# Quarter loads of two MLP weights, and engine orders written out as lists, in a fused attention and MLP kernel

## The chip, the cores and the metric

The kernel runs on one core of a Trainium2 chip. The metric is the device time of one execution in microseconds (us); for a kernel that was run several times it is the median. A profile is one execution recorded by the hardware profiler. PE is the matrix engine (TensorE), with a queue of its own for weight loads (PEld); ACT, DVE and POOL are the scalar, vector and GpSimd engines; SP is the sync engine, which here issues nearly all DMA transfers, one after another in its queue.

## The reference

Input x has 2048 rows of 448. Two branches are computed from it and mixed by a gate per row.

```python
g = sigmoid((x * gate_w).sum(-1, keepdims=True))
a = attention(x, wq, wk, wv, beta) @ wo      # 16 heads of 28, 4 segments of 512 rows, masked softmax,
                                             # mixed with a linear memory of the segments before
h = layernorm(x)
u = gelu(einsum('bsd,sf->bdf', h, w1) + b1)  # w1: 2048 x 1792
y = einsum('bdf,fs->bds', u, w2) + b2        # w2: 1792 x 2048
out = g * a + (1 - g) * y.transpose(0, 2, 1)
```

The MLP mixes rows, not columns: its weights w1 and w2 run over the 2048 rows. They are some 7.3 MB each and are the largest inputs.

## The kernel before

**Two products.** `mm1(ft)` (lines 1055 to 1080) computes one of 14 blocks of 128 hidden units: 16 matmuls named u{ft}-0 to u{ft}-15, one for each tile of 128 rows of x, summed in one bank of PSUM; ACT and DVE then apply the gelu. `mm2(T)` (lines 1082 to 1098) computes one of 16 blocks of 128 output rows: 14 matmuls y{T}-0 to y{T}-13 over the hidden blocks; DVE mixes the result with the attention branch and SP writes it out. The last block is split in two by columns.

**The ring of slots.** Weights come through three slots in SBUF of 4096 columns each. `ring_load` (lines 569 to 584) fills the next one: loads w1_0 to w1_6 bring 256 columns of w1 for all 16 row tiles (1024 KB in pieces of 512 bytes, enough for two values of ft), loads w2_0 to w2_7 bring 256 columns of w2 for all 14 tiles (896 KB, two values of T). Each load is one DMA with one semaphore of its own. A slot has one resource, `R_slot[r]` (line 517): a load waits until the last matmul that reads the slot's former content is through, and the first matmul of a chain waits until the whole load has landed. The w1 loads also wait, by `reads=R_wv` (line 578), for the load of wv.

**Other traffic in SP's queue.** SP also issues the loads of x and of the other weights, transposes of x from DRAM (line 538), transposes of phi(k) within SBUF (line 781, named tk), and the gathers of the fourth group of heads: `gather` writes rows of the projected k and q to a scratch tensor in DRAM, spare_heads (line 755, names gk and gq), and reads them back into other partitions (line 760). The scores of a segment's last heads need the rows read back; for the first two segments these reads are gq0_h0, gk0_h0, gk0_h1, gq0_h1 and gq0_h2, and the first scores that wait for them are sc1_2 (line 954).

**Attention.** `scores` fills the banks 0 to 3 with logits (line 954, names sc), ACT takes their exponential (line 963), POOL masks them (line 966). `pv_unit` computes a unit's product with v (line 990, names pv) and, behind the first segment, the memory's product (names mem); DVE transposes both out of PSUM (line 1004 for mem, named tm; line 1006 for pv, named ta). ACT's line 816 (named gt) reads the gate's column from the bank of the v projection (names prt).

**The order of the work.** Every operation is recorded by `Sched.op` with what it reads and writes. `Sched.plan` (lines 157 to 278) then simulates the engines with given costs and priorities (shifted by the table SHIFTS) and so sets the order of each engine's instructions and the bank that each user of the four free PSUM banks (4 to 7) gets: the one that came free first. `finalize` (line 280) works out the waits: an instruction waits for the engines and DMAs that it depends on, unless an earlier wait of its engine implies that. A wait beyond the first of an instruction is an instruction of its own (line 323). In a run of matmuls that holds one on 32 columns, the matmuls of 128 columns are issued as four of 32 columns (lines 329 to 333).

Of the kernel before, what the change touches and what calls it, by code (L numbers as in the profile page):

```python
# [17 lines left out]
NT = 16  # L18
# [3 lines left out]
NFT = 14  # L22
# [41 lines left out]
SWITCH = 97.0  # L64
# [10 lines left out]
class Sched:  # L75
# [13 lines left out]
    def op(self, eng, fn, reads=(), writes=(), name=None, dma=False, out=False, cost=100.0, prio=0.0, mode="f",  # L89
           nbytes=0, rel=0.0, port=False, take=None, use=(), alt=None,  # L90
# [27 lines left out]
        if dma:  # L118
            self._dma_uid += 1
            o.evspace = "dma_u%d" % self._dma_uid  # L120
            o.is_event = True
# [35 lines left out]
    def plan(self, shifts=()):  # L157

        import bisect

        shifts = dict(shifts)
        for o in self.ops:
            o.prio = (o.prio[0] + shifts.get(o.name.split("-")[0], 0.0), o.idx)
        succ = [[] for _ in self.ops]
        left = [0] * len(self.ops)
        ready = [o.rel for o in self.ops]
        for o in self.ops:
            for d in {x.idx: x for x in o.deps + o.order}.values():
                succ[d.idx].append(o)
                left[o.idx] += 1  # L170
        free = {e: 0.0 for e in ENGINES}
        mode = "f"
        chan = 0.0
        port = 0.0
        waiting = {e: [] for e in ENGINES}
        avail = {e: [] for e in ENGINES}
        banks = {p: {b: (0.0, []) for b in v} for p, v in self.pool.items()}
        for p, v in self.later.items():
            banks[p].update({b: (1e18, []) for b in v})

        def push(o):
            for e in o.alts:
                bisect.insort(waiting[e], (ready[o.idx], o.prio, o))

        for o in self.ops:
            if left[o.idx] == 0:
                push(o)
        line = []
        while len(line) < len(self.ops):
            best = None  # L190
            for e in ENGINES:
                w, a = waiting[e], avail[e]
                t = free[e]
                while w and w[0][0] <= t:
                    _, p, o = w.pop(0)
                    if o.start is None:
                        bisect.insort(a, (p, o))
                a[:] = [x for x in a if x[1].start is None]
                w[:] = [x for x in w if x[2].start is None]
                while True:  # L200
                    pick = None
                    can = [o for p, o in sorted(a + [(x[1], x[2]) for x in w if x[0] <= t])
                           if not o.take or sum(v[0] <= t for v in banks[o.take[0].pool].values()) >= len(o.take)]
                    if can:
                        pick = can[0]
                        if e == "PE":

                            if mode != "f":
                                lead = [o.prio for o in can if o.tile == "f"][:1]
                                tiled = [o for o in can if o.tile == "r" or o.tile == "h" and ([o.prio] <= lead or not lead)]  # L210
                                tiled = [o for o in tiled if o.tile == mode] + tiled
                                pick = tiled[0] if tiled else pick
                            elif pick.tile == "h":
                                rest = [o for o in can if o.tile == "f"]
                                if rest and not any(o.tile == "r" for o in can) and t < ready[pick.idx] + pick.hold:
                                    pick = rest[0]
                        break
                    nxt = [x[0] for x in w if x[0] > t][:1]
                    if a or w:
                        nxt += [v[0] for p in banks.values() for v in p.values() if t < v[0] < 1e12]  # L220
                    if not nxt:
                        break
                    t = min(nxt)
                if pick is not None and (best is None or t < best[0]):
                    best = (t, e, pick)
            t, e, o = best
            for g in o.take:
                pool = banks[g.pool]
                b = min((v[0], b) for b, v in pool.items())[1]
                g.bank = b  # L230
                o.deps = o.deps + pool[b][1]
                pool[b] = (1e18, [])
            o.eng = e
            o.fn, c, pt = o.alts[e]
            if o.evspace is None:
                o.evspace = e
            if e == "PE" and t < COLD:
                c *= 2.0
            if e == "PE" and o.tile != mode:
                c += SWITCH  # L240
                mode = o.tile
            if pt:
                t = max(t, port)
                port = t + c
            o.start = t
            o.cost = c
            free[e] = t + c
            if o.nbytes:
                chan = max(chan, t + 1090.0) + o.nbytes / 290.0
                o.end = max(t + 1900.0, chan + 850.0)  # L250
            else:
                o.end = t + c + LAT[e]
            for g in o.free:
                g.left -= 1
                g.users.append(o)
                if g.left == 0:
                    banks[g.pool][g.bank] = (max(x.end + hop(x.eng, "PE") for x in g.users), g.users)
            o.pos = len(line)
            line.append(o)
            self.per_eng[e].append(o)  # L260
            for x in succ[o.idx]:
                isdep = any(d is o for d in x.deps)
                r = (o.end + min(hop(e, y) for y in x.alts)) if isdep else free[e]
                if ready[x.idx] < r:
                    ready[x.idx] = r
                left[x.idx] -= 1
                if left[x.idx] == 0:
                    push(x)
# [9 lines left out]
        return max(o.end for o in line)  # L278
# [69 lines left out]
def pool_cost(n):  # L348
# [5 lines left out]
SHIFTS = (  # L354
# [29 lines left out]
def build_kernel(nc, X, WQ, WK, WV, WO, BETA, W1, B1, W2, B2, GW, OUT):  # L384
# [839 lines left out]
```

## Time and profile before

| what | us |
|---|---|
| median of 3 runs | 178.38 |
| lowest and highest run | 178.17, 179.44 |
| the profiled execution | 178.57 |
| its span, first to last instruction | 176.8 |
| PE busy | 169.7 |
| DVE busy | 149.6 |
| ACT busy | 134.1 |
| POOL busy | 69.2 |

The granted PE clock was 1.000 over the span. The profile's page gives the busy time and number of instructions of each engine, the DMA issues with their time to landing, and groups of instructions by source line. Other views of the trace are a table of busy time by stretch of time, a list of who waited for whom, and the timeline. In the list of waits a row reads: engine and line that stood idle, after the arrow what released it, then total us, number of waits and the longest. In the timeline a row reads: start, duration, engine, line, operation, tiles written and read, number of instructions merged into the row, and idle time before it with its releaser. A q behind an engine's name means its queue: an issue or a wait, not computation. A DMA's duration in SP's timeline is the time that the queue was held by issuing it; its landing is told apart from that.

### The profile page before, as it was taken

The page shows a single profiled execution, that of the slowest core. Times are in us where ns is not written, and L with a number is a line of the kernel's source. Part 1 is how long each engine was busy: PE and PEld are TensorE (multiplying, and loading weights), DVE is VectorE, ACT ScalarE, POOL GpSimd, SP SyncE. Part 2 cuts the span into 40 slices and gives each one's busy share as a digit, 9 for nine tenths or more (in the row PEclk, how much of TensorE's full clock was granted, in tenths as well). Part 3 has the DMA queues.
Part 4 walks back from the last instruction along what each step waited for, and adds up shares of the span by engine and source line. Part 5 has one row for each costly group of instructions (what it writes and reads, how often), then busy time and mean ns, then how long its engine had stood idle before and what let it go on. Part 6 is the DMA issues. An engine that isn't in the chain of part 4 may idle for free.

```text
span 176.8 us, 5552 instructions
## 1 busy us (share of the span) xinstructions
PE 169.7 (96%) x2354; PEld 81.8 (46%) x2354; DVE 149.6 (85%) x337; ACT 134.1 (76%) x170; POOL 69.2 (39%) x93
## 2 busy tenths in 40 slices
PE   8699999999999999999999999999999999999993
PEld 3343443345544544444544344444444544555652
DVE  6499999799995898998999999997889999992222
ACT  2277898999689999999999999987878877405100
POOL 8003016542302233437745644359474425450000
PEclk9999999999999999999999999999999999999999
DMA  6979983699939915852007360203938600166511
GB/s 153 281 142 304 259 158 84 167 302 193 245 78 268 240 35 161 192 171 46 4 11 201 77 170 22 61 28 95 224 99 227 170 8 4 56 176 194 153 59 52
DMA packets 49752, 24.62 MB, mean 139 GB/s; under 512 B 14256, under 2 KB 49488, under 8 KB 49728
## 3 DMA queue, kind: packets, MB, share of 16 engines
q1 hardware_dynamic: 49440, 24.05, 56.6%
q8 instruction: 18, 0.29, 0.7%
q10 hardware_dynamic: 288, 0.23, 0.6%
q14 instruction: 6, 0.05, 0.1%
HBM read 18.76 MB, written 2.36 MB: 119 GB/s over the span
## 4 chain that ended last, share of the span: by engine, by line
PE 78%; ACT 6%; DVE 6%; DMA 4%; SPq 3%; issue 2%
PE t L332 67%; PE t L954 6%; PE t L990 4%; DMA t<-in_A_wk_dram 3%; ACT t L963 2%; SPq L760 1%; SPq L755 1%; DVE t L913 1%; PE t L840 1%; DMA t<-spare_heads 1%; ACT t L1076 1%; ACT t L1065 1%; ACT t L1047 1%; DVE t L1071 1%; DVE t L1073 1%
## 5 line engine op out<-in xcount | busy, mean ns | idle before, releaser
L332 PE MATMUL t<-t 128*32 128x448 bf16 (+10 forms) x1620 | 145.8, 347 | 2.8 <-DVE t L649 1.7
L332 PEld LDWEIGHTS t<-t 128*32 128x32 bf16 (+2 forms) x1620 | 66.6, 97 | 68.6 <-issue 15.1
L963 ACT ACTIVATE t<-t 128x2048 bf16<-128x2048 f32 x40 | 76.2, 1904 | 6.3 <-PE t L954 6.1
L966 POOL TENSOR_SCALAR_AFFINE_SELECT t<-t 128x512 bf16<-128x512 bf16 x64 | 46.8, 732 | 58.2 <-ACT t L963 54.4
L1093 DVE SCALAR_TENSOR_TENSOR t<-t 128x448 bf16<-128x448 f32 (+2 forms) x17 | 10.9, 653 | 12.8 <-PE t L332 12.8
L1021 POOL TENSOR_TENSOR t<-t 128x448 bf16<-128x448 f32 x12 | 14.6, 1219 | 9.7 <-DVE t L1019 9.1
L1047 ACT ACTIVATE t<-t 128x448 bf16<-128x448 f32 x12 | 8.5, 732 | 10.3 <-PE t L332 10.1
L954 PE MATMUL t<-t 28*128 28x512 bf16 (+3 forms) x256 | 15.8, 301 | 0.3 <-DMA t<-spare_heads 0.3
L906 POOL TENSOR_TENSOR t<-t 128x4 f32<-128x4 f32 x4 | 4.5, 1130 | 20.9 <-DVE t L904 20.9
L1006 DVE STREAM_TRANSPOSE t<-t 128x512 f32<-128x512 f32 x16 | 11.2, 701 | 0.9 <-PE t L990 0.9
L990 PE MATMUL t<-t 128*32 128x256 bf16 (+3 forms) x256 | 11.5, 299 | 0.4 <-ACT t L816 0.4
L954 PEld LDWEIGHTS t<-t 28*128 28x128 bf16 x256 | 4.5, 92 | 14.1 <-ACT t L963 6.9
L1027 DVE STREAM_TRANSPOSE t<-t 128x512 bf16<-128x512 bf16 x16 | 10.9, 687 | 0.0
L1073 DVE SCALAR_TENSOR_TENSOR t<-t 128x448 f32<-128x448 f32 x14 | 8.8, 636 | 1.5 <-ACT t L1068 1.5
L1076 ACT ACTIVATE t<-t 128x448 f32<-128x448 f32 x14 | 8.5, 612 | 1.8 <-DVE t L1073 1.8
L1065 ACT ACTIVATE t<-t 128x448 f32<-128x448 f32 x14 | 9.3, 674 | 0.7 <-PE t L332 0.7
L1078 DVE SCALAR_TENSOR_TENSOR t<-t 128x448 bf16<-128x448 f32 x14 | 9.6, 695 | 0.0
L897 DVE BATCH_NORM_STATS2 t<-t 128x6 f32<-128x448 bf16 x16 | 9.4, 608 | 0.1
L1017 DVE SCALAR_TENSOR_TENSOR t<-t 128x448 f32<-128x448 f32 x12 | 9.2, 776 | 0.1
L990 PEld LDWEIGHTS t<-t 128*32 128x32 bf16 x256 | 6.9, 97 | 5.0 <-ACT t L816 0.7
L1004 DVE STREAM_TRANSPOSE t<-t 128x512 f32<-128x512 f32 x12 | 8.4, 698 | 0.4
L778 DVE SCALAR_TENSOR_TENSOR t<-t 128x512 bf16<-128x512 bf16 x12 | 8.4, 708 | 0.0
(69 smaller groups left out, 144.3 us busy)
## 6 DMA issues: line engine op xcount, KB each, us to landing
t<-in_B_w_dram SPq DMA_DIRECT2D x7, 1024.0 KB, 7.1
t<-in_B_w_dram SPq DMA_DIRECT2D x8, 896.0 KB, 5.3
out_dram<-t SPq DMA_DIRECT2D x15, 112.0 KB, 2.4
t<-in_A_x_dram SPq DMA_DIRECT2D x3, 448.0 KB, 4.8
t<-in_A_wo_dram SPq DMA_DIRECT2D x4, 98.0 KB
t<-in_A_wq_dram SPq DMA_DIRECT2D x1, 336.0 KB, 5.5
t<-in_A_wv_dram SPq DMA_DIRECT2D x1, 336.0 KB, 5.7
spare_heads<-t SPq DMA_DIRECT2D x8, 32.0 KB
```

What stands on the lines that cost most here:

```text
L332: last = e.matmul(out[q], w[:, q], x, skip_group_check=True, **kw)
L954: last = e.matmul(bank(hl)[:, c0 : c0 + w], kT[r, hg, s * 512 + j * 128 : s * 512 + j * 128 + 128], qT[r, hg, s * 512 + 128 * j : s * 512 ...
L963: op("ACT", lambda e: e.activation(pslot(g), ps[:, 0:4, :], ACT.Exp, scale=SCALE), reads=R_bank[0:4], writes=[g.res], take=g, name=f"exp{p ...
L966: op("POOL", lambda e, c0=c0: e.affine_select(pslot(g)[:, :, c0 : c0 + 128], pslot(g)[:, :, c0 : c0 + 128], pattern=[[0, 4], [1, 128]], co ...
L990: last = e.matmul(bank(cb)[32 * hl : 32 * hl + 32, 128 * j : 512], vaug[:, 4 * s + j, 32 * h : 32 * h + 32], pslot(P_fill[u // 2][f])[:, h ...
L1006: dv(lambda e: e.transpose(t2[:, 0, :], bank(cb)[:, 0:512]), [bres(cb)], [R_tt[tb][0]], "ta", 630, use=(cb,))
L1021: op("POOL", lambda e: e.tensor_tensor(o3, n3[0], n3[1], op=ALU.add), reads=R_tt[tb], writes=[R_ob[tb]], name=f"o{u}", cost=1280, port=Tru ...
L1027: dv(lambda e: e.transpose(oT[:, hg, s * 512 : s * 512 + 512], o), [R_ob[tb]], qres(hg, s), "ot", 635)
L1047: op("ACT", lambda e: e.activation(ag(T), bank(b)[:, 0:D], ACT.Identity, bias=b2g[:, T : T + 1], scale=gcol[:, T : T + 1]), **buse(b), rea ...
L1065: op("ACT", lambda e: e.activation(gg[:, q, :], bank(b)[:, 0:D], ACT.Square, bias=b1s[:, ft : ft + 1], scale=math.sqrt(GC)), **buse(b), re ...
L1073: op("DVE", lambda e: e.scalar_tensor_tensor(gg[:, q, :], gg[:, q, :], 1.0, vh[:, q, :], op0=ALU.add, op1=ALU.mult), reads=[R_gg[q], R_vh[ ...
L1093: op("DVE", lambda e: e.scalar_tensor_tensor(outst[:, p, c0:c1], bank(b)[:, 0 : c1 - c0], omg[:, T : T + 1], ag(T)[:, c0:c1], op0=ALU.mult ...
```

## The change

Each load of w1 and w2 is issued as up to four DMAs, one for each four of the 16 (w1) or 14 (w2) tiles; w2's last part has two. A slot has four resources instead of one, and each has a semaphore that the slot's loads share over time (12 semaphores instead of 15). The matmul for tile t reads part t // 4 of the slot alone. The dependence of the w1 loads on wv is gone. So 60 loads stand where 15 stood.

`plan` no longer simulates anything: it reads for each engine a list of names, ORDER, in which `u0-0@4*7` stands for seven operations from u0-0 on, the first of which takes bank 4. In SP's list the four parts of a load follow one another where the load stood. SHIFTS is gone.

```diff
-    def plan(self, shifts=()):
...
+    def plan(self, order):
+        seen, ops = {}, {}
         for o in self.ops:
...
+            k = seen[o.name] = seen.get(o.name, -1) + 1
+            ops[o.name + (f"#{k}" if k else "")] = o
+        held = {(g.pool, g.bank): g for o in self.ops for g in o.free if g.bank is not None}
+        queue = {}
...
+        while any(queue.values()):
+            n = len(line)
             for e in ENGINES:
...
+                while queue[e] and ready(*queue[e][0]):
+                    o, banks = queue[e].pop(0)
+                    assert len(banks) == len(o.take)
+                    for g, b in zip(o.take, banks):
+                        g.bank = int(b)
+                        last = held.get((g.pool, g.bank))
+                        o.deps = o.deps + (last.users if last else [])
+                        held[g.pool, g.bank] = g
...
-SHIFTS = (
...
+ORDER = {
+    "PE": """
...
+wo1@5 wo0#1@6 wo2@4 sc3_0 wo3@7 lot8@64 prt8 prt9 mem5@7 sc3_1 pv5@7 u10-0@6*6 sc3_2 lot10@57 prt10 prt11 mem6@4
...
+    "SP": """
+ldx0 ldwk1 ldwk0@0 ldx2 ldwq0@1 ldwqb ldwv0 ldwvb ldb2 ldgw ldgwb dtx1_0 ldwo1 dtx1_1 ldx4 ldx8 ldx12 ldbeta ldb1
+ldw1_0_0 ldw1_0_1 ldw1_0_2 ldw1_0_3 tk0_1 dtx2_0 dtx2_1 ldwo0 ldwo2 ldwo3 gk0_1 gk0_2 gk0_3 gq0_0 gq0_2 gq0_3 tk0_0
+dtx3_1 ldw1_1_0 ldw1_1_1 ldw1_1_2 ldw1_1_3 ldw1_2_0 ldw1_2_1 ldw1_2_2 ldw1_2_3 gq0_1 gk0_0 dtx3_0 ldw1_3_0 ldw1_3_1
+ldw1_3_2 ldw1_3_3 tk0_2 gk2_0 gk2_1 gk2_2 gk2_3 gq0_h0 gk0_h0 gk0_h1 gq0_h1 gq0_h2 ldw1_4_0 ldw1_4_1 ldw1_4_2
...
-    R_slot = R("slot", NSL)
+    R_slot = [R(f"slot{i}_", 4) for i in range(NSL)]
...
-            op("SP", lambda e: e.dma_start(slots[r].rearrange("p (t f) -> p t f", t=NT),
-                                           w1v[:, :, k * 256 : k * 256 + 256]),
-               reads=R_wv, writes=[R_slot[r]], name=f"ldw1_{k}", dma=True, cost=500,
-               nbytes=1320000, prio=(-2.5, -0.5)[k] if k < 2 else 0)
...
+        for part in range(4):
+            t = slice(4 * part, min(4 * part + 4, NT if k < 7 else NFT))
+            n = t.stop - t.start
+            dst = slots[r][:, 256 * t.start : 256 * t.stop].rearrange("p (t f) -> p t f", t=n)
+            src = w1v[:, t, k * 256 : k * 256 + 256] if k < 7 else w2v[:, t, (k - 7) * 256 : (k - 7) * 256 + 256]
+            op("SP", lambda e, dst=dst, src=src: e.dma_start(dst, src), writes=[R_slot[r][part]],
+               name=f"ldw1_{k}_{part}" if k < 7 else f"ldw2_{k - 7}_{part}", dma=True, cost=500, nbytes=82000 * n,
+               prio=(-2.5, -0.5)[k] if k < 2 else 0, space=f"dma_s{r}_{part}")
...
-               reads=[R_slot[fb % NSL], R_x[st]], writes=[bres(b)], take=b if st == 0 else None, name=f"u{ft}-{st}", mode="x", cost=pe_cost(448),
+               reads=[R_slot[fb % NSL][st // 4], R_x[st]], writes=[bres(b)], take=b if st == 0 else None, name=f"u{ft}-{st}", mode="x", cost=pe_cost(448),
...
-               reads=[R_slot[r]] + (R_uT if ft == 0 else [R_uT[ft]]), writes=[bres(b)] + ([] if ft else [R_wo_y[T]]),
+               reads=[R_slot[r][ft // 4]] + (R_uT if ft == 0 else [R_uT[ft]]), writes=[bres(b)] + ([] if ft else [R_wo_y[T]]),
...
-    sch.plan(SHIFTS)
+    sch.plan(ORDER)
```

More of the change, by code (lines that the diff above doesn't have):

```diff
@@ L89, in op @@
     def op(self, eng, fn, reads=(), writes=(), name=None, dma=False, out=False, cost=100.0, prio=0.0, mode="f",
-           nbytes=0, rel=0.0, port=False, take=None, use=(), alt=None,
+           nbytes=0, rel=0.0, port=False, take=None, use=(), alt=None, space=None,
            hold=HOLD):
@@ L155, in op @@
         return o
-    def plan(self, shifts=()):
-        import bisect
-        shifts = dict(shifts)
+    def plan(self, order):
+        seen, ops = {}, {}
         for o in self.ops:
[L163 to L190, printed above, removed]
-            for e in ENGINES:
[L192 to L268, printed above, removed]
@@ new lines, in plan @@
+            k = seen[o.name] = seen.get(o.name, -1) + 1
+            ops[o.name + (f"#{k}" if k else "")] = o
+        held = {(g.pool, g.bank): g for o in self.ops for g in o.free if g.bank is not None}
+        queue = {}
+        for e in ENGINES:
+            queue[e] = []
+            for word in order[e].split():
+                word, _, n = word.partition("*")
+                word, _, banks = word.partition("@")
+                stem, _, first = word.rpartition("-")
+                for k in range(int(n or 1)):
+                    queue[e].append((ops.pop(f"{stem}-{int(first) + k}" if n else word), banks))
+                    banks = ""
@@ new lines, in plan, with ready @@
+        assert not ops
+        line, done = [], set()
+        def ready(o, banks):
+            users = [held.get((g.pool, int(b))) for g, b in zip(o.take, banks)]
+            return all(d.idx in done for d in o.deps + o.order) and all(g is None or g.left == 0 for g in users)
+        while any(queue.values()):
+            n = len(line)
+            for e in ENGINES:
+                while queue[e] and ready(*queue[e][0]):
[6 more added lines that the diff above has]
+                        held[g.pool, g.bank] = g
+                    o.eng = e
+                    o.fn = o.alts[e][0]
+                    o.evspace = o.evspace or e
+                    for g in o.free:
+                        g.left -= 1
+                        g.users.append(o)
+                    o.pos = len(line)
+                    done.add(o.idx)
+                    line.append(o)
+                    self.per_eng[e].append(o)
+            assert len(line) > n
@@ L277, in plan @@
                 run.append(o)
-        return max(o.end for o in line)
     def finalize(self):
@@ new lines @@
+pv0@6 u0-15 u1-12*4 prk2_1 sc1_0 u2-0@6*6 pv1@7 u2-6*4 sc1_1 u2-10*6 u3-0@4*16 u4-0@5*16 u5-0@7*2 u6-0@6*14 sc1_2
+u6-14*2 u5-2*12 sc1_3 u5-14*2 u7-0@4*3 pv2@5 u8-0@6*5 sc1_4 u8-5*10 mst0@5 sc2_0 u8-15 u7-3*4 pv3@7 u7-7*4 sc2_1
+u7-11*5 loq2_0@57 prq2_0 prq2_1 u9-0@6 sc2_2 u9-1*3 loq2_2@57 prq2_2h mem4@4 u9-4*5 sc2_3 u9-9*7 prq2_2 pv4@4 sc2_4
+wo1@5 wo0#1@6 wo2@4 sc3_0 wo3@7 lot8@64 prt8 prt9 mem5@7 sc3_1 pv5@7 u10-0@6*6 sc3_2 lot10@57 prt10 prt11 mem6@4
+u10-6*5 sc3_3 mst1@5 u10-11*5 u11-0@4*2 pv6@5 sc3_4 u11-2*14 u13-0@6 sc4_0 u13-1*7 mem7@5 pv7@4 u13-8 sc4_1 u13-9*7
@@ new lines @@
+phq2_2 rec8 oa9 oa8 fin2 om9 mk2_3 om8 fin1 ot9 phk2_3 ta10 fin4 ot8 tm10 tm11 eps10 ta11 eps11 rec10 rec11 oa10
+om10 fin5 oa11 msta2 ot10 mstc2 mstc2#1 mstc2#2 fin3 mstc2#3 om11 mq3_0 mq3_2 cpv13 ot11 gcol3 phq3_0 ta12 omg3
+ta13 tm12 b2g3 phq3_2 eps12 mq3_1 rec12 phq3_1 oa12 om12 tm13 mq3_3 eps13 ot12 rec13 tm14 om13 phq3_3 eps14 oa13
+ta14 fin8 fin6 ot13 rec14 oa14 tm15 ta15 eps15 om14 fin9 rec15 oa15 om15 fin10 ot14 ot15 fin7 fin14 fin11 fin12
+fin13 fin15 fin15#1""",
+    "POOL": """
+szg id0 z3_0 id1 z3_1 v0 mhalf v1 szb rstd0 rstd4 mask0_0_0 rstd8 mask0_1_1 mask0_1_3 rstd12 mask0_2_2 mask0_2_2#1
```

58 lines of the change are left out of this document (50 added, 8 removed), and 28 rows, old and new, of the table SHIFTS.

## The prediction

> **What bounds the kernel now.** I read the page's head and DMA issues first, then the table of busy time by stretch, then the list of what the matrix engine (PE) waited for, and only then the timelines of SP and of two places on PE.
>
> ```profile
> span 176.8 us, 5552 instructions
> PE 169.7 (96%) x2354; PEld 81.8 (46%) x2354; DVE 149.6 (85%) x337; ACT 134.1 (76%) x170; POOL 69.2 (39%) x93
> t<-in_B_w_dram SPq DMA_DIRECT2D x7, 1024.0 KB, 7.1
> t<-in_B_w_dram SPq DMA_DIRECT2D x8, 896.0 KB, 5.3
> ```
>
> PE is busy 96% of the span, so PE bounds the kernel; only what lengthens or fills PE's idle time can move the end. The 15 loads that change are the last two rows: 7 of w1 and 8 of w2, landing in the median 7.1 and 5.3 us after issue. The next rows, from the table by stretch, give stretch and length, then PE's busy time and instructions, the other engines, clock, DMA share and GB/s.
>
> ```profile
> 8.00:32.00 24.00, 23.64 (x149) 9.91 (x147) 22.79 (x81) 20.24 (x41) 6.27 (x7) 1.00 0.89 185
> 32.00:53.00 21.00, 20.50 (x218) 9.74 (x216) 19.85 (x47) 18.06 (x25) 5.83 (x9) 1.00 0.96 202
> ...
> 62.00:65.00 3.00, 2.72 (x60) 1.42 (x60) 2.93 (x9) 3.00 (x5) 1.51 (x2) 1.00 0.17 41
> ...
> 74.00:81.00 7.00, 6.34 (x59) 2.67 (x54) 7.00 (x12) 7.00 (x10) 3.10 (x5) 1.00 0.49 140
> 81.00:110.00 29.00, 29.00 (x446) 13.51 (x434) 28.15 (x54) 29.00 (x37) 16.55 (x20) 1.00 0.31 81
> 110.00:150.00 40.00, 40.00 (x564) 19.02 (x564) 37.37 (x76) 32.38 (x32) 21.66 (x27) 1.00 0.42 101
> 150.00:174.00 24.00, 24.00 (x568) 14.35 (x560) 12.87 (x23) 5.00 (x6) 4.71 (x6) 1.00 0.42 122
> ```
>
> From 81 to 174 us PE has no idle time at all, at a granted clock of 1.00. Two things follow: a delay of PE before 81 us is never made up, and all idle time between 8 and 174 us is 0.36 + 0.50 + 0.28 + 0.66 = 1.8 us (the two stretches left out are full). What ended PE's idle times:
>
> ```profile
> PE t L332 <- DVE t L649: 1.7, 1, 1.7
> PE t L638 <- PEq L1209: 0.8, 1, 0.8
> PE t L990 <- ACT t L816: 0.4, 1, 0.4
> PE t L954 <- DMA t<-spare_heads: 0.3, 1, 0.3
> PE t L332 <- issue: 0.3, 1, 0.3
> PE t L332 <- ACT t L791: 0.3, 1, 0.3
> ...
> ```
>
> The two rows left out name ACT and DVE, 0.2 us each. No row names in_B_w_dram: PE never stood waiting for a weight load. That is the main reading. A finer semaphore lets a matmul start on a quarter of a slot, but there is no such wait to shorten.
>
> **The change, part by part.**
>
> (1) Waits on PE by quarter. Where u or y chains had one wait per slot they get four. The price is bounded by two rows, PE's extra wait instructions and a stretch of PE with two slot changes (u4-0, u6-0) and several waits in it:
>
> ```profile
> L323 PEldq EVENT_SEMAPHORE  x59: 51/51/992, 2.3 to 165.5; - x59
> 42.17 10.39 PE L332 MATMUL t<-t 128*128 128x448 bf16 x54
> ```
>
> A wait that needs an instruction of its own takes 51 ns; 45 more of them, none hidden, would be 2.3 us. But the 54 matmuls run at 10.39/54 = 0.19 us each, waits included: PE's queue looks ahead while the matmul before still streams. I take zero; that cover is gone only where PE is idle already. The 45 more increments on PE's side end such matmuls too and cost nothing by the same row.
>
> (2) Earlier writes. The last quarter of a load still waits for the slot's last reader, so SP is held there exactly as long as before, and what is queued behind it (gq2, gk3, out1, gq3) is released no earlier by that wait. The other three can be issued some matmuls sooner.
>
> ```profile
> SPq L582 <- PE t L332: 25.4, 8, 8.8
> ```
>
> SP stood 25.4 us before the eight w2 loads, so their additional issues fall into time in which SP waited anyway. PE does not wait for them; worth zero.
>
> (3) The dropped wait of w1's loads on wv:
>
> ```profile
> 4.24 0.49 SPq L532 DMA_DIRECT2D t<-in_A_wv_dram  x1
> t<-in_A_wv_dram SPq DMA_DIRECT2D x1, 112.0 KB, 5.6
> 13.82 0.39 SPq L576 DMA_DIRECT2D t<-in_B_w_dram  x1
> ```
>
> wv's second part lands at 4.24 + 5.6 = 9.8 us, the first w1 load is issued at 13.82: the wait was over, zero.
>
> (4) More issues on SP ahead of the gathers. This is where the change could hurt. SP's queue runs without a pause to 51.3 us, and at its end stand the five reads of spare_heads (L760) for which scores sc1_2 waits: PE's 0.3 us row. The loads w1_0 to w1_3 stand ahead of them, so 12 more issues do. One costs 0.39 us as above plus some 0.04 between, 12 x 0.43 = 5.2 us, if nothing hides it. SP's rows at these loads (start, duration):
>
> ```profile
> 14.26 5.79 SPq L781 DMA_TRANSPOSE t<-t  x1
> ...
> 32.58 1.53 SPq L576 DMA_DIRECT2D t<-in_B_w_dram  x1
> 34.15 3.43 SPq L755 DMA_DIRECT2D spare_heads<-t  x1
> ...
> 40.85 1.60 SPq L576 DMA_DIRECT2D t<-in_B_w_dram  x1
> 42.50 3.18 SPq L781 DMA_TRANSPOSE t<-t  x1
> 45.73 2.17 SPq L755 DMA_DIRECT2D spare_heads<-t  x4
> 48.09 1.59 SPq L760 DMA_DIRECT2D t<-spare_heads  x1
> 51.02 0.30 SPq L760 DMA_DIRECT2D t<-spare_heads  x1
> ...
> 54.46 2.52 SPq L781 DMA_TRANSPOSE t<-t  x2
> ```
>
> A transpose normally takes SP 2.52/2 = 1.26 us and a gather write 2.17/4 = 0.54; right behind a w1 load they take 5.79, 3.43 and 3.18. As I read it, SP is held until enough of the load's data has drained: by 4.5 us after w1_0, 1.1 after w1_1 (w1_2 itself, 1.53 against 0.39), 2.9 after w1_2 and 1.9 after w1_3. Three more issues take 1.3 us. They fit into each hold but the second, which is 0.2 short, and the next hold has 1.6 us to spare for that. The bytes to drain are the same, so the end of each hold stays. The ends for this term: +5.2 us if the holds absorb nothing, and -0.3 us if the reads land early enough to close PE's gap. I take +0.1, near the bottom, since every hold is about as long as what it has to hide or longer.
>
> (5) Quarters as transfers. If each paid a landing time of its own, the loads would slow. Rows: landing of three x loads of 448 KB (issued from 11.07 to 12.24, by the same view), of w1_1 and w1_2, and of the first x tiles of 112 KB on a quiet queue:
>
> ```profile
> DMA to landing us min/median/max: 4.0/4.8/5.6
> DMA to landing us min/median/max: 6.4/8.4/10.4
> DMA to landing us min/median/max: 2.5/2.6/2.7
> ```
>
> The first x load lands at 11.07 + 4.0 = 15.1 and the third at 12.24 + 5.6 = 17.8, so 1.35 us apart, half of what even 112 KB takes alone: queued transfers overlap their landing time. I take zero. [...]
>
> (6) The written lists are not quite as they were. On all five engines they name the order that the planner of before makes, but the PSUM banks differ in 61 places. Most of these exchange two banks that are both empty by then, and the list of PE's waits shows one wait for a bank at most, pv5's. One does not: the new list has mem5@7, sc3_1, pv5@7, where before's planner put mem5 into bank 4 and pv5 into bank 6.
>
> ```profile
> 79.92 0.70 DVE L1004 STREAM_TRANSPOSE t<-t 128x512 f32<-128x512 f32 x1
> 80.24 0.21 ACT L816 ACTIVATE t<-t 128x1 f32<-128x1 f32 x1
> 80.50 0.73 PE L990 MATMUL t<-t 128*32 128x512 bf16 x16 [0.41 <-ACT t L816]
> ```
>
> pv5 (L990) now starts when ACT's L816 has left bank 6, at 80.45 us, plus 0.05. In the new list it waits for the transpose of mem5 out of bank 7 (DVE, 80.62) and starts at about 80.67: +0.17 us, in front of the stretch that makes nothing up. The bounds are zero, if DVE comes to that transpose earlier, and +0.4, its idle time once more.
>
> **The sum.** The profiled execution took 178.57 us (span 176.8 and 1.77 around it). 178.57 + 0 + 0 + 0 + 0.1 + 0 + 0.17 = 178.84. That execution lies 0.19 above the median of 178.38, so against the median the forecast is 178.65, say 178.7 us.
>
> **The rivals.** A measurement of this kernel can tell about 1%, 1.8 us, from no change.
>
> *SP is late with the gathers (slower).* Place: the reads of spare_heads at L760, then PE at sc1_2. If the holds are not drain time but a cost that each load's issue triggers, the 12 issues come on top: +5.2, 183.9 us; with half of them exposed 181.3. It decides beyond 1% once more than four issues (1.7 us) are exposed. For it: SP has no pause to 51.3 us, and nothing behind 53 us gives time back. Against it: a load on a quiet stretch takes 0.39 us itself, and only what follows a load is long.
>
> *Quarters land one by one (slower).* Four landings of at least 2.5 us are 10 us, against (32.58 + 10.4) - (31.95 + 6.4) = 4.6 us between the landings of w1_1 and w1_2, w1_1 being issued at 31.95. Four loads ahead of the gathers give 4 x 5.4 = 21.6 us, 200 us. The x rows speak against it. [...]
>
> *The finer loads do help (faster).* The reads land sooner, PE's 0.3 us gap before sc1_2 closes, and 178.65 - 0.1 - 0.3 = 178.25 us is left: still no change that could be told. For more than 1%, all of the 1.8 us of idle time would have to go, most of which waits for ACT, DVE and instruction issue, not for loads.
>
> **How the numbers follow.** My forecast 0.74; loads help a little 0.08; all idle time goes 0.04; SP late 0.12; one by one 0.02. So within 1% 0.82, slower 0.14, faster 0.04. The likeliest case by itself spans 178.0 (the gap closed, and a little of the runs' own spread) to 179.4 (the slowest run shown of before); the range reaches into the first rival with four to five issues exposed, 180.6, and leaves out some 0.16.
>
> **What would show it.** Right: PE busy near 169.7 us, no PE wait that names in_B_w_dram, 60 load issues near 0.4 us, transposes and gathers behind them shorter than 5.79, 3.43 and 3.18 by what the quarters took, the last L760 read issued near 51.0, and pv5's idle time grown from 0.41 to about 0.6 with DVE L1004 as releaser. Wrong: the last L760 read much after 51.0 and PE's wait for spare_heads above 0.5 us; a PE wait for in_B_w_dram; matmuls of a u chain further apart than 0.19 us.

## The result and the profile after

The changed kernel takes 177.05 us (median of 20 runs, 176.6 to 178.2) beside 177.97 us for the kernel before (20 runs, 177.17 to 179.44). The ratio is 0.9954, with a 95% interval of 0.9934 to 0.9973: 0.46% faster, surely a gain, and inside the 1% that the forecast called no change. But 177.05 lies under the forecast of 178.7 and under the low end of its range, 178.0, and the time fell where the forecast had it rise a little, from 178.38 to 178.65. The profiled execution took 177.03 us. (Ratios leave out runs over 1.5% above a kernel's fastest and so are not the quotients of the medians; medians and ranges hold all runs.)

The head of the page of after and its weight loads:

```profile
span 175.3 us, 5601 instructions
PE 169.6 (97%) x2354; PEld 82.0 (47%) x2354; DVE 149.3 (85%) x337; ACT 133.7 (76%) x170; POOL 69.3 (40%) x93
...
t<-in_B_w_dram SPq DMA_DIRECT2D x52, 256.0 KB, 4.1
...
t<-in_B_w_dram SPq DMA_DIRECT2D x8, 128.0 KB, 3.8
```

PE's work is the same, 169.6 us against 169.7; the span is 1.5 us shorter, so all of it is PE's idle time and the ends of the span. What ended PE's idle times in after:

```profile
PE t L608 <- PEq L1179: 0.8, 1, 0.8
PE t L264 <- DVE t L619: 0.7, 1, 0.7
PE t L264 <- DVE t L883: 0.6, 1, 0.6
PE t L960 <- DVE t L974: 0.6, 1, 0.6
PE t L264 <- ACT t L761: 0.3, 1, 0.3
PE t L264 <- ACT t L701: 0.2, 1, 0.2
```

Line numbers of after are 30 to 68 lower (L332 is L264 here, L990 L960, L1004 L974). No row names in_B_w_dram, as before. Three rows are gone, the wait of scores for spare_heads, the 0.3 us of "issue" and a wait of 0.2 us for DVE (L919). The first wait (L619, wk's arrival at the start) fell from 1.7 to 0.7 us, of which a new one (L883, 0.6) gives part back; both vary between executions of one kernel (a second profile of the changed kernel, after_again below, has no row of the first and 1.2 us for L883), and PE's warm-up matmuls fill a part of that time (the last five, L638 in before, 4.34 to 5.59 us, with the 1.67 us of idle time behind them). The table by stretch, same columns as in the prediction:

```profile
32.00:53.00 21.00, 20.44 (x219) 9.75 (x219) 20.07 (x48) 17.86 (x25) 5.41 (x8) 1.00 0.94 215
...
62.00:65.00 3.00, 3.00 (x57) 1.40 (x49) 2.93 (x9) 3.00 (x5) 0.92 (x1) 1.00 0.08 21
...
81.00:110.00 29.00, 29.00 (x430) 13.45 (x423) 27.90 (x56) 29.00 (x38) 16.18 (x19) 1.00 0.28 77
```

The stretch from 62 to 65 us, 2.72 us of PE before, is now full. What stood there before, in PE's timeline of before:

```profile
61.05 0.67 PE L840 MATMUL t<-t 128*32 128x32 bf16 x64
61.65 0.40 PE L954 MATMUL t<-t 28*128 28x512 bf16 x4
61.97 0.93 PE L332 MATMUL t<-t 128*32 128x448 bf16 x14
63.19 0.56 PE L332 MATMUL t<-t 128*32 128x448 bf16 x6 [0.28 <-issue]
...
64.98 0.40 PE L954 MATMUL t<-t 28*128 28x384 bf16 x8
```

And in after:

```profile
60.46 0.67 PE L810 MATMUL t<-t 128*32 128x32 bf16 x64
61.06 0.40 PE L924 MATMUL t<-t 28*128 28x512 bf16 x4
61.38 1.13 PE L264 MATMUL t<-t 128*32 128x448 bf16 x20
...
63.74 0.40 PE L924 MATMUL t<-t 28*128 28x384 bf16 x8
```

Between the two L924 rows (L954 before) lies the same work. It took 64.98 - 61.65 = 3.33 us before and 63.74 - 61.06 = 2.68 us after: 0.65 us gone, more than the 0.28 that the row calls idle, since the modelled ends of the matmuls cover the rest. I call this the stall; its length is that distance less 2.68.

The second place is the end. The program ends with waits for all its outputs. The last eight in SP's queue, in before and then in after (number, shortest, median and longest duration in ns, first and last start):

```profile
L1184 SPq EVENT_SEMAPHORE  x8: 28/28/28, 175.9 to 176.3; - x8
```

```profile
L1154 SPq EVENT_SEMAPHORE  x8: 28/28/28, 173.7 to 174.8; - x8
```

Before, the first of the eight is for the last output: it ends at 175.9, seven more follow at 0.06 us each, and the span ends 0.9 us behind it (176.8). After, the last output is waited for last, at 174.8, and the span ends 0.5 us behind (175.3): 0.4 us. The cause is in a line that the diff does not touch, `for sp2 in sorted(sch.out_spaces)`, which sorts the semaphores' names as text. In before the outputs were DMAs number 93 to 109, and as text dma_u100 to dma_u109 come ahead of dma_u93; the additional loads moved the numbers to three digits, and the text order became the order of issue.

Comparing the start of each operation's weight load in the two traces, from 8 us on, these are the steps that stay: -0.22 us from the first waits (wk's arrival and what it shifts), -0.36 at sc1_2 (its wait for spare_heads), -0.64 at the stall, +0.17 at pv5, -0.06 at a later matmul; then -0.4 at the end: together -1.5, the difference of the spans. These are two single executions: the medians differ by 0.92 us only, and the experiments below show which steps belong to the change.

### The profile page after: what moved, and what is told of

Same layout as the page of the kernel before. It is cut to its first block, busy times and chain, and to the rows that moved or that the text cites. A ratio compares the mean times of both kernels' runs of the same rounds, so it can differ in the third digit from the quotient of the medians.

```text
span 175.3 us, 5601 instructions
## 1 busy us (share of the span) xinstructions
PE 169.6 (97%) x2354; PEld 82.0 (47%) x2354; DVE 149.3 (85%) x337; ACT 133.7 (76%) x170; POOL 69.3 (40%) x93
## 4 chain that ended last, share of the span: by engine, by line
PE 89%; DVE 5%; DMA 3%; ACT 1%; SPq 0%; issue 0%
PE t L264 76%; PE t L924 7%; PE t L960 5%; DMA t<-in_A_wk_dram 3%; PE t L810 1%; DVE t L1048 1%; DVE t L987 0%; DVE t L883 0%; ACT t L701 0%; DVE t L703 0%; DVE t L1041 0%; ACT t L1035 0%; DVE t L1021 0%; DVE t L974 0%; DVE t L976 0%
## 5 line engine op out<-in xcount | busy, mean ns | idle before, releaser
L264 PE MATMUL t<-t 128*32 128x448 bf16 (+10 forms) x1620 | 145.3, 346 | 1.9 <-DVE t L619 0.7
L264 PEld LDWEIGHTS t<-t 128*32 128x32 bf16 (+2 forms) x1620 | 66.5, 97 | 67.1 <-issue 13.3
L924 PE MATMUL t<-t 28*128 28x512 bf16 (+3 forms) x256 | 15.8, 301 | 0.0
L960 PE MATMUL t<-t 128*32 128x512 bf16 (+3 forms) x256 | 11.3, 299 | 0.6 <-DVE t L974 0.6
L924 PEld LDWEIGHTS t<-t 28*128 28x128 bf16 x256 | 4.5, 92 | 13.8 <-ACT t L933 7.4
L1035 ACT ACTIVATE t<-t 128x448 f32<-128x448 f32 x14 | 9.1, 656 | 1.1 <-PE t L264 1.1
L1046 ACT ACTIVATE t<-t 128x448 f32<-128x448 f32 x14 | 8.2, 598 | 1.5 <-DVE t L1043 1.5
L960 PEld LDWEIGHTS t<-t 128*32 128x32 bf16 x256 | 6.8, 97 | 5.4 <-DVE t L974 0.8
L974 DVE STREAM_TRANSPOSE t<-t 128x512 f32<-128x512 f32 x12 | 8.4, 697 | 0.4
L989 DVE TENSOR_TENSOR t<-t 128x448 f32<-128x448 f32 x12 | 8.2, 685 | 0.0
```

What stands on the lines that cost most here:

```text
L264: last = e.matmul(out[q], w[:, q], x, skip_group_check=True, **kw)
L924: last = e.matmul(bank(hl)[:, c0 : c0 + w], kT[r, hg, s * 512 + j * 128 : s * 512 + j * 128 + 128], qT[r, hg, s * 512 + 128 * j : s * 512 ...
L960: last = e.matmul(bank(cb)[32 * hl : 32 * hl + 32, 128 * j : 512], vaug[:, 4 * s + j, 32 * h : 32 * h + 32], pslot(P_fill[u // 2][f])[:, h ...
```

## The experiments

Two theories stood at first. *The loads take the stall away*: the "issue" row is PE out of instructions, and loads in quarters let the next piece of its program through. *The lists do it*: new banks and written orders move PE's work. The end of the program was tried by itself. All times below are against the kernel before on the same chip, five rounds each.

**c_whole**: the changed kernel with whole loads.

```diff
-ldw1_0_0 ldw1_0_1 ldw1_0_2 ldw1_0_3 tk0_1 ...
+ldw1_0 tk0_1 ...
...
-    R_slot = [R(f"slot{i}_", 4) for i in range(NSL)]
+    R_slot = R("slot", NSL)
...
```

> The changed kernel with whole loads again (15 DMAs, one resource per slot, the w1 loads waiting on wv as before), but with the written lists and their banks. Theory 'loads' (the gain comes from the quarters: gathers that land sooner and a PE that does not run dry at 62.9 us): pv5's 0.17 us is all that is left, so 0.1 to 0.3 us slower than before, ratio 1.001; the profile has PE's 0.3 us wait for spare_heads and the 0.3 us of issue near 63 us again, and about 0.87 us from the last landing to the end of the span. Theory 'lists' (the gain comes with the written lists and banks): ratio near 0.995 as the whole change.

**q_old_banks**: the changed kernel with before's 61 bank digits in PE's list.

```diff
-... mem5@7 sc3_1 pv5@7 ...
+... mem5@4 sc3_1 pv5@6 ...
```

> The changed kernel with the banks of before in its list of PE, nothing else. Theory 'bank' (pv5 waits for the transpose of mem5 because both take bank 7): pv5 starts 0.17 us sooner after sc3_1, its idle time goes from 0.6 back to 0.4 us with ACT's line of the gate column as releaser, and the time is 0.17 us below the changed kernel, ratio to before about 0.9945. Rival (the wait only moves to the next bank): PE's idle time near 80 us stays at 0.6 us in sum and the ratio at 0.9954.

**b_tail**: the kernel before, its final waits in the order of number.

```diff
-for sp2 in sorted(sch.out_spaces):
+for sp2 in sorted(sch.out_spaces, key=lambda n: int(n[5:])):
```

> The kernel before with one line changed: SP's final waits for the outputs in the order of the outputs' numbers, not of their names as text. Theory 'tail' (in before the waits for the last output come first and eight wait instructions of some 0.06 us stand behind them; renumbering the DMAs happens to put them last): the time from the last landing to the end of the span falls from 0.87 to 0.5 us and the time by 0.38 us, ratio 0.998, nothing else moves. Rival (the end of the span is set by something else): ratio 1.000.

**q_late_tail**: the changed kernel, the last outputs' waits first again.

```diff
-for sp2 in sorted(sch.out_spaces):
+for sp2 in sorted(sch.out_spaces, key=lambda n: int(n[5:]))[7:] + sorted(sch.out_spaces, key=lambda n: int(n[5:]))[:7]:
```

> The changed kernel with the final waits turned back so that those for the last output come first, as they stand in before. Theory 'tail': 0.38 us slower than the changed kernel, ratio to before about 0.9975, and 0.87 us from the last landing to the end of the span. Rival (the tail is worth nothing, all of the gain is in the loads): ratio 0.9954 as the changed kernel.

Measured: c_whole 178.4 us, ratio 0.9999 [0.9969, 1.0029]; q_old_banks 177.04, 0.9927 [0.9894, 0.9961]; b_tail 178.37, 0.9986 [0.9959, 1.0014]; q_late_tail 177.33, 0.9942 [0.9911, 0.9972]. PE's timeline of c_whole shows the stall, 64.25 - 60.64 - 2.68 = 0.93 us:

```profile
60.64 0.40 PE L923 MATMUL t<-t 28*128 28x512 bf16 x4
60.97 0.93 PE L264 MATMUL t<-t 128*32 128x448 bf16 x14
62.46 0.56 PE L264 MATMUL t<-t 128*32 128x448 bf16 x6 [0.56 <-issue]
...
64.25 0.40 PE L923 MATMUL t<-t 28*128 28x384 bf16 x8
```

So lists and banks give nothing that these runs could tell: their theory asked for 0.995, and the interval begins at 0.9969. Both kernels in quarters have no stall. b_tail has 1.26 us of it, which hides its shorter end from a single profile. The ends themselves follow the order of the waits alone, in b_tail (span 176.5) and q_late_tail (span 175.8):

```profile
L1184 SPq EVENT_SEMAPHORE  x8: 28/28/28, 174.9 to 176.0; - x8
```

```profile
L1154 SPq EVENT_SEMAPHORE  x8: 27/28/28, 174.9 to 175.3; - x8
```

In b_tail the end comes 0.5 us behind the last wait's start, which is the last output's; in q_late_tail the last output's wait comes first, 0.9 us ahead of the end. That 0.4 us is shown in the traces; b_tail's ratio agrees with it (0.4 of 178.65 would be 0.9978), but its interval also holds no gain at all. q_late_tail's ratio does not show it: the theory asked for 0.9975, the rival for 0.9954, and the measured 0.9942 is under both, with 0.9975 just outside its interval. Its median is 0.29 us above that of q_old_banks on the same chip, where the end and the banks together would make 0.57. So what the end is worth in whole runs is not shown. The banks cost what the prediction said; pv5 in after and in q_old_banks:

```profile
79.44 0.73 PE L960 MATMUL t<-t 128*32 128x512 bf16 x16 [0.56 <-DVE t L974]
```

```profile
79.18 0.73 PE L960 MATMUL t<-t 128*32 128x512 bf16 x16 [0.39 <-ACT t L786]
```

Next question: which load? At 57 us, 4 to 6 us ahead of the stall, SP issues w1_5; its row in before:

```profile
57.02 0.58 SPq L576 DMA_DIRECT2D t<-in_B_w_dram  x1
```

**c_only5**: whole loads, w1_5 alone in quarters (from here on every kernel with whole loads has its final waits in the order of number, unless named otherwise, and the new banks).

```diff
+QUARTERS = ('ldw1_5',)
```

> Whole loads, written lists and new banks, final waits by number, and w1_5 alone in quarters. Up to 81 us the matrix engine's (PE's) instructions are those of the kernel with whole loads. Theory 'w1_5' (PE's next instructions are fetched by a DMA that is held up while the whole w1_5 load, issued at 57 us, is in the DMA queue, so PE runs dry behind mst0 at 62 to 64 us; quarters let the fetch in): PE is busy 3.00 us from 62 to 65, against 2.72 in before, the fetch near 60 us starts 1 us sooner, and the ratio to before is about 0.9935 (stall 0.9, final waits 0.4, pv5 -0.1). Rival 'position' (the quarters' additional PE waits shift where in PE's program the fetches fall): the stall stays, ratio 0.998.

**q_whole5**: the changed kernel with w1_5 alone whole.

```diff
-ldw1_5_0 ldw1_5_1 ldw1_5_2 ldw1_5_3 tk1_1 ...
+ldw1_5 tk1_1 ...
```

> The changed kernel with w1_5 alone as one whole load. Theory 'w1_5': the stall of 0.6 to 1.2 us near 62 us is back, ratio to before about 0.999 to 1.000. Rival 'position': PE's additional waits ahead of 62 us are all still there, so no stall, and the ratio stays near 0.9954. Third theory 'all loads' (every load gives a little): ratio about 0.996.

**c_late5**: whole loads, w1_5 issued behind the transpose tk1_1 (at 66.45 us in its profile).

```diff
-ldw1_5 tk1_1 ldw1_6 ...
+tk1_1 ldw1_5 ldw1_6 ...
```

> Whole loads, written lists and new banks, final waits by number, and w1_5 issued behind the transpose tk1_1 (65.7 us) instead of ahead of it; its first reader runs at 81 us. PE's program is word for word that of the kernel with whole loads. Theory 'w1_5': no whole load is in flight near 60 us, the stall near 62 us is gone without any quarter, ratio about 0.9935. Rival 'position': the stall stays, ratio about 0.998. It could come back in another place, with w1_5 and w1_6 one behind the other from 67 us on; then PE's idle time shows it there.

**after_again**: the changed kernel as it is, on this chip.

> The changed kernel once more, unaltered, to stand beside the others on the same chip and for a second profile of it. Theory 'w1_5' and its rivals all expect a ratio of 0.994 to 0.997; a second profile without PE idle time from 62 to 65 us speaks for a stall that the change removes each time, one with idle time there for chance.

Measured: c_only5 177.08 us, 0.9945 [0.9916, 0.9974]; q_whole5 176.88, 0.9944 [0.9916, 0.9971]; c_late5 176.85, 0.9954 [0.9924, 0.9985]; after_again 177.06, 0.9947 [0.9921, 0.9974]. None has the stall, and the forecast 0.9935 of c_only5 and c_late5 lies within both intervals. c_late5 has no quarter load at all and loses it by the place of one load:

```profile
61.17 0.39 PE L932 MATMUL t<-t 28*128 28x512 bf16 x4
61.49 1.13 PE L264 MATMUL t<-t 128*32 128x448 bf16 x20
...
63.85 0.40 PE L932 MATMUL t<-t 28*128 28x384 bf16 x8
```

But q_whole5 speaks against "a whole w1_5 makes the stall": it was to come back and did not. Quarters of the other loads also add waits to PE's program (24 wait instructions ahead of 57 us instead of 21), which might move the places at which the program is fetched. So "place" became the rival of "queued load".

**c_num**: all loads whole, the base of the others.

```diff
+QUARTERS = ()
```

> Loads whole, lists and banks of the changed kernel, final waits in the order of number. It is the base of the other three. Theory 'queued load' (PE's next stretch of program is delayed when the whole w1_5, 1 MB, is in the queue at 57 to 61 us) and theory 'place' (the instructions that quarters add on PE move the point at which the program is fetched): both expect PE's idle time of the kind issue near 62 to 64 us, 0.6 to 1.2 us, a last transfer to end of span of 0.5 us, and a ratio of 0.997 to 1.000. Theory 'chance' (the stall comes and goes between executions whatever the loads): it may be missing here, and then it may come back in any of the others.

**c_only0**: w1_0 alone in quarters, 24 waits ahead of 57 us, w1_5 whole.

```diff
+QUARTERS = ('ldw1_0',)
```

> As the base, but w1_0 alone, the load that is 30 us away from the stall, in quarters: PE gets some of the waits that quarters add ahead of 57 us, and the queue at 57 to 61 us is the base's, with the whole w1_5. Theory 'queued load' expects the stall as in the base (0.6 to 1.2 us) and the base's ratio, within 0.002. Theory 'place' expects it gone or cut to under 0.3 us and a ratio 0.003 to 0.005 below the base's.

**q_whole45**: the changed kernel, w1_4 and w1_5 whole.

```diff
-ldw1_4_0 ldw1_4_1 ldw1_4_2 ldw1_4_3 gk2_h0 ...
+ldw1_4 gk2_h0 ...
```

> The changed kernel with w1_4 and w1_5 whole, all other loads in quarters: PE has its added waits ahead of 57 us, and the queue from 50 to 61 us holds whole loads only. Theory 'place' expects no stall near 62 to 64 us and the ratio of the changed kernel, 0.994 to 0.996. Theory 'queued load' in its wider form (the quarters of w1_4, not only those of w1_5, leave room in the queue) expects the stall back, 0.6 us or more, and a ratio of 0.997 to 1.000.

**c_late5_old**: c_late5 with before's banks.

> No quarters at all: whole loads, w1_5 issued behind the transpose tk1_1 at about 65.7 us in place of 57, final waits in the order of number, and before's PSUM banks. If quarters are needed only because they keep the queue free at 57 to 61 us, this reaches what quarters with the old banks reached, a ratio of 0.991 to 0.994, with no stall and a pv5 wait of 0.4 us. If quarters give something more, it stays at 0.995 or above.

Measured: c_num 178.08 us, 1.0001 [0.9972, 1.0031]; c_only0 178.16, 0.9974 [0.9933, 1.0014]; q_whole45 177.64, 0.9946 [0.9908, 0.9985]; c_late5_old 177.18, 0.9939 [0.9913, 0.9965]. The stalls are 0.31, 0, 1.75 and 0 us. c_num's is half of the least that was expected, and it has no idle row of its own; only the distance of the two rows of scores, 64.29 - 61.30 = 2.99 us, shows it:

```profile
61.30 0.40 PE L932 MATMUL t<-t 28*128 28x512 bf16 x4
...
64.29 0.40 PE L932 MATMUL t<-t 28*128 28x384 bf16 x8
```

q_whole45's timeline, with "place" as much in its favour as in the changed kernel:

```profile
60.90 0.39 PE L936 MATMUL t<-t 28*128 28x512 bf16 x4
61.23 0.75 PE L264 MATMUL t<-t 128*32 128x448 bf16 x12
63.54 0.56 PE L264 MATMUL t<-t 128*32 128x448 bf16 x8 [1.56 <-issue]
...
65.33 0.40 PE L936 MATMUL t<-t 28*128 28x384 bf16 x8
```

"Place" alone therefore falls. c_only0 looks like a point for it, but its runs lie in two heaps, five from 176.79 to 177.26 us, one at 177.96 and six from 178.37 to 179.79 (four of these up to 179.08): its one profile came from the lower heap. q_whole45's runs are spread as far (176.75 to 179.76), half of them under 177.65, so that its ratio is as low as "place" asked for.

The last four asked whether w1_4 and w1_5 must both be whole.

**c_only4**: w1_4 alone in quarters.

```diff
+QUARTERS = ('ldw1_4',)
```

> Whole loads, final waits in the order of number, the changed kernel's lists and banks; w1_4 alone, issued near 50.5 us, is in quarters, w1_5 is whole. Theory 'two whole loads' (the stall needs w1_4 and w1_5 both whole in the queue between 50 and 61 us): no stall in the profile, runs within 176.5 to 177.7 us, ratio 0.992 to 0.996. Theory 'only w1_5 counts': the stall as in the base without quarters, 0.3 to 1.2 us, runs spread to 179 us, ratio 0.998 to 1.001.

**c_only6**: w1_6 alone in quarters, issued behind the stall.

```diff
+QUARTERS = ('ldw1_6',)
```

> The same, but w1_6 alone in quarters, a load that is issued behind the stretch in question. Both theories expect the stall as in the base without quarters (0.3 to 1.2 us), runs spread from 177 to 179 us, ratio 0.998 to 1.001. If it is gone here too, what helps is not the queue at 50 to 61 us, and both theories fall.

**q_old_again** and **late5_again**: q_old_banks and c_late5_old once more, on one chip.

> The changed kernel (all loads in quarters) with before's PSUM banks, once more: no stall, pv5 wait 0.4 us, ratio 0.991 to 0.995. It is the measure for the next one on the same chip.

> No quarters, w1_5 issued behind tk1_1, final waits in the order of number, before's banks, once more: if quarters are worth only the stall, its ratio is within 0.002 of that of the kernel in quarters with the same banks; if quarters do something more, it is 0.003 or more above.

Measured: c_only4 177.75 us, 0.9961 [0.9928, 0.9994]; c_only6 178.23, 0.9964 [0.9928, 1.0]; q_old_again 177.36, 0.9923 [0.9884, 0.9961]; late5_again 176.81, 0.9896 [0.9854, 0.9938]. c_only4 keeps a stall of 0.31 us, so the theory of two whole loads falls as well: w1_5 alone can make it. c_only6, with both theories expecting the stall, has 1.60 us, though its ratio came out under the 0.998 that both asked for:

```profile
60.99 0.40 PE L933 MATMUL t<-t 28*128 28x512 bf16 x4
61.31 0.93 PE L264 MATMUL t<-t 128*32 128x448 bf16 x14
63.48 0.56 PE L264 MATMUL t<-t 128*32 128x448 bf16 x6 [1.24 <-issue]
...
65.27 0.40 PE L933 MATMUL t<-t 28*128 28x384 bf16 x8
```

**What ties them together.** The page of after counts the transfers of instructions in a DMA queue of their own:

```profile
q8 instruction: 18, 0.29, 0.8%
```

They are 18 transfers of 16384 bytes in every trace. The fourth one falls near 60 us (60.69 in before, 57.83 in after). The table gives how long it starts ahead of the 28x512 row above (the row behind the burst of 64 matmuls on 128x32), and the stall:

| kernel | w1_5 | starts ahead, us | stall, us | runs, us |
|---|---|---|---|---|
| before | whole | 0.96 | 0.65 | 177.17 to 179.44 |
| c_whole | whole | 0.89 | 0.93 | 177.43 to 179.15 |
| b_tail | whole | 0.55 | 1.26 | 177.41 to 178.81 |
| c_num | whole | 1.31 | 0.31 | 177.59 to 179.33 |
| c_only4 | whole | 1.40 | 0.31 | 177.27 to 178.98 |
| c_only6 | whole | 0.07 | 1.60 | 177.03 to 179.05 |
| q_whole45 | whole | -0.15 | 1.75 | 176.75 to 179.76 |
| c_only0 | whole | 1.84 | 0 | 176.79 to 179.79 |
| q_whole5 | whole | 1.84 | 0 | 176.52 to 177.44 |
| c_only5 | quarters | 1.92 | 0 | 176.57 to 177.5 |
| q_old_banks | quarters | 2.11 | 0 | 176.8 to 178.58 |
| after_again | quarters | 2.90 | 0 | 176.53 to 177.61 |
| q_late_tail | quarters | 3.06 | 0 | 177.01 to 179.22 |
| after | quarters | 3.23 | 0 | 176.6 to 178.2 |
| q_old_again | quarters | 3.34 | 0 | 176.78 to 178.42 |
| c_late5_old | later | 2.91 | 0 | 176.65 to 177.59 |
| late5_again | later | 3.03 | 0 | 176.52 to 177.68 |
| c_late5 | later | 3.15 | 0 | 176.7 to 177.62 |

One rule fits all 18 profiles: the stall is about 1.66 us less the lead, and zero from there on (c_num: 1.66 - 1.31 = 0.35 against 0.31; q_whole45: 1.81 against 1.75; the largest miss is 0.16, in c_whole). The 1.66 is fitted to the seven stalls; that the other eleven, with leads of 1.84 and more, have none was not put into it. With w1_5 out of the queue the transfer leads by 2.9 to 3.15 us; with it in quarters by 1.9 to 3.3; with it whole by 1.84 at the most. c_num and c_late5 share PE's program up to there, and differ in the place of w1_5 alone: 1.31 and 3.15.

The traces show where PE stands, and where it is when the transfer starts, if its weight loads are counted from the start of the program. All seven stalls come behind the 597th (the 596th in q_whole45, which has three more wait instructions ahead of it): PE stops at one place of its program. In the seven profiles with a lead of 2.89 us or more the transfer starts behind weight load 467 (463 in q_old_again), with 23 or 24 wait instructions ahead of 57 us as with 21. That is 130 weight loads and 130 matmuls ahead of the place of the stall. So the waits that quarters add hardly move the start of the transfer, and "place" is not needed to explain a late transfer. In the other eleven profiles the transfer starts behind weight loads 487 to 583.

What lies between is the load. w1_5 is moved as 2048 packets of 512 bytes. Ahead of the transfer start 691 to 1963 of them in the nine profiles with w1_5 whole; 333 to 1033 in four of the six with it in quarters; and none with it later. So by these profiles the queued load is what makes the program late (a lead of 1.31 us in c_num with the load in the queue, 3.15 in c_late5 without it), and the late program is what PE waits for. In the two quarter profiles that are left, after and q_old_again, the transfer starts before the load's first packet: there it was early, and the quarters were not put to the test. With w1_5 whole the lead falls on either side of the edge at 1.66 us; that it does so from one execution to the next is likely from the spread of the runs, but no such kernel was profiled twice.

Not settled: what sets how many packets go ahead, 691 to 1963 for the same whole load; and why q_whole5's eleven runs stay narrow while c_only0's twelve, with the same lead in the profile, do not.

The version without quarters (w1_5 behind tk1_1, waits by number, before's banks) beats the kernel before on both chips (0.9939 and 0.9896). It is no slower than quarters with the same banks on the one chip that ran both (0.9896 against 0.9923, a little more than the 0.002 that was expected, with overlapping intervals). It was not run beside the changed kernel itself, whose 0.9954 and 0.9947 were taken elsewhere.

## Why the prediction was right and wrong

(1), (2), (3), (5) right: waits by quarter, earlier writes, the wait on wv and the quarters as transfers cost PE nothing that the traces show. Of the 45 additional waits only four became instructions of their own (63 in after, 59 before). The same 54 matmuls with their slot changes took the same time to the last digit in after, and the scores sc1_2 now follow at once:

```profile
41.95 10.39 PE L264 MATMUL t<-t 128*128 128x448 bf16 x54
52.27 0.40 PE L924 MATMUL t<-t 28*128 28x256 bf16 x8
```

(4) right in that the holds hide the issues, 0.1 us too dear, and wrong on the issues themselves: they took 0.51 us in the median and up to 1.65, not "near 0.4". SP's timeline of after:

```profile
13.57 3.00 SPq L552 DMA_DIRECT2D t<-in_B_w_dram  x4
16.61 3.10 SPq L751 DMA_TRANSPOSE t<-t  x1
...
31.95 5.16 SPq L552 DMA_DIRECT2D t<-in_B_w_dram  x8
37.15 1.08 SPq L725 DMA_DIRECT2D spare_heads<-t  x2
...
41.26 2.22 SPq L552 DMA_DIRECT2D t<-in_B_w_dram  x4
43.53 1.20 SPq L751 DMA_TRANSPOSE t<-t  x1
...
47.33 3.27 SPq L730 DMA_DIRECT2D t<-spare_heads  x5
```

The transpose behind w1_0 takes 3.10 us instead of 5.79 and ends at 19.71, against 14.26 + 5.79 = 20.05 before; behind w1_3 it ends at 44.73, against 45.68. The holds took in all twelve issues, and the five reads are through at 50.60 us, against 51.02 + 0.30 = 51.32 before. The gap at sc1_2 closed, but it closed in all 17 later profiles, with whole loads too (c_num, b_tail): it belonged to the one execution that I read, and "the finer loads help" at this place is not supported.

(6) right: pv5 lost 0.17 us, as forecast to the hundredth, released by DVE's transpose, and before's banks give it back.

The sum failed, in three terms. First, its starting point: 178.38 was the median of three runs and 177.97 that of twenty, 0.41 us less; a stall that differs between executions would spread such runs. Second, and this is the step that failed, the sentence that the 1.8 us of idle time "waits for ACT, DVE and instruction issue, not for loads". The row "PE t L332 <- issue" was quoted and its stretch, 0.28 us, added up, but "issue" was taken as something that no load can touch. By the 18 profiles it is PE waiting for its program behind a load (in before the transfer leads by 0.96 us, in the kernels with no stall by 1.84 or more), and it is longer than the idle time that the rows show: 0.65 us in the profile of before. Between medians on one chip it is 178.08 - 177.18 - 0.17 for the banks = 0.73 us from c_num to c_late5_old, and 178.40 - 177.33 = 1.07 us from c_whole to q_late_tail, which end alike and differ in the quarters and the wait on wv. Third, the final waits had no term: -0.4 us by the traces. 178.65 - 0.41 - 0.1 - 0.73 - 0.4 = 177.01, against 177.05 measured. The -0.1 is the charge of (4). That this comes out within 0.04 us is luck: with 1.07 in place of 0.73 it would be 176.67, and the 0.4 is not shown in whole runs.

The chance of 0.82 on "within 1%" went to the right case, but not for its reasons, and that is luck too: a loss of 0.17 us stood against two gains that the prediction did not see, and they happened to be small. The range was wrong at its low end because every term without a row was bounded by costs of loads and waits, and none by the idle rows that had no engine's name to them.

## What to carry to other kernels

An "issue" gap on a busy engine may be its program arriving late (here 0.31 to 1.75 us in seven of 18 profiles): look for the instruction transfers in the DMA queues, and at which large load is in the queue a few us ahead of a burst of short instructions. Moving or splitting that one load can be worth as much as splitting all (c_late5 0.9954 and c_only5 0.9945 beside 0.9947 for the whole change on one chip), so try one load before a ring. And look at both ends of the span too: what the program waits for last, and in which order, is time of the kernel.

## What the runs showed of the hardware

PE goes on about 1.5 us after the record of its instruction transfer ends (1.34 to 1.56 in the seven profiles with a stall); that transfer takes 0.9 to 1.7 us for 16 KB. In the seven profiles with the longest leads (2.90 to 3.34 us) it starts some 130 weight loads and as many matmuls ahead of the place where PE stalls in others; when a 1 MB load is being moved it starts up to some 3 us later (a lead of -0.15 us in q_whole45, against 2.91 to 3.15 with that load issued later). Eight wait instructions in a row, all for outputs that have landed when the first of them is through, stand 0.06 us apart on SP (L1184 in before, 28 ns each, from 175.90 to 176.34 us). Behind w1_0, what SP issues next is through 6.2 us after the load's first issue in before, where the load is one DMA, and 6.1 us after it in after, where it is four. Behind w1_3 the same takes 4.8 us before and 3.5 after. So in these two places four DMAs hold SP no longer than one does.
